# Loads of q, k and v of batches 1 to 3 by casting DMAs of GpSimd, in an attention and feed-forward kernel

## The chip, the cores and the metric

The kernel runs on one core of a Trainium2 chip. The metric is the device time of one execution in microseconds (us). The engines are named as the profile names them: PE multiplies matrices and transposes through the identity, DVE is the vector engine, ACT the scalar engine, POOL is GpSimd, SP only issues DMAs. A letter q behind a name (SPq) means the engine's instruction queue.

## The reference

Inputs are q, k, v of shape (4, 8, 768, 64) and two weight matrices, all float32. Attention is causal and keeps, for each query, the 6 chunks of 32 keys with the largest upper bound; its output goes through a feed-forward layer with softplus.

```python
k_min, k_max = k_chunks.min(axis=3), k_chunks.max(axis=3)       # 24 chunks of 32 keys
ub = np.sum(np.maximum(q * k_min, q * k_max), axis=-1)          # bound for each chunk
ub = np.where(causal, ub, -1e9)
top_chunks = np.argsort(ub, axis=-1)[..., -6:]
scores = q @ k.T / sqrt(64)
scores = np.where(sel & causal_pos, scores, -1e9)               # sel: chunk among the 6
attn = exp(scores - max) / sum
x = (attn @ v), heads side by side                              # (3072, 512)
out = softplus(x @ w_in) @ w_out                                # w_in (512, 2048), w_out (2048, 512)
```

## The kernel before

Work goes by units. A unit is a pair of heads with a range of query tiles of 128 rows: batch 0 has units 0 to 3 (first halves of the four pairs, 3 tiles) and 4 to 7 (second halves); batches 1 to 3 have units 8 to 19, one whole pair (6 tiles) each, so that unit u from 8 on is pair u - 4. For each unit there are small steps, and the whole order of these steps is written out by hand in the strings of ORDER (lines 21 to 60): "start" goes from the first load to the feed-forward input of batch 1, "cycle" is run twice, with the unit numbers raised by 4 the second time; steps of units over 19 fall away. There is no scheduler: each engine gets its instructions in the order of the text, takes them one after the other, and waits where it has to. The words that matter here:

- L8.k, L8.q, L8.v: load (line 165). Lu.c starts the DMA of one input of unit u. Units from 8 on bring 384 KB in one DMA on SP's queue (line 178) as float32 into a staging tile (three of each kind), in pieces of 64 numbers (256 bytes): for each of the 128 partitions 12 pieces, 6 tiles by 2 heads.
- ck, cq, cv: cast_k, cast_q, cast_v (lines 185 to 206). They turn the staging tile into bfloat16: k and q into kb and qb (three buffers each), v into a vaug tile. The letter behind it is the engine: V is DVE, A is ACT, G or nothing is GpSimd.
- vaug (line 113): five tiles that hold v as bfloat16 with a column of ones for the sums. Pair p uses tile p % 5, thus unit 8 (pair 4) and unit 13 (pair 9) use the same one.
- fk, fq: turn (line 212), a transposing DMA on SP's queue from kb or qb to kT_sb or qT_sb. kr, qr copy its rows into the operands Kaug and Qaug; rg, pk, qp, qn, U, M, T find the bounds and the selected chunks (DVE mostly), and s puts the selection into Qaug.
- S (scores, line 351): S8.1.0 is unit 8, head 1, group 0 of its score blocks: matmuls on PE, then Exp on ACT (line 366); for group 0 GpSimd then masks the diagonal blocks with an affine_select (line 369).
- V (values, line 373): V8.0 is unit 8, head 0: PE multiplies the weights attnT with vaug (line 383). n divides by the sums on DVE, X transposes on PE, x copies into xT.
- I and F: feed-forward input (line 413, softplus on ACT) and output (line 433). They are spread between the attention steps of the next batch and keep PE busy. ob copies the result to SBUF and stores it.
- w: the weights, in six casting DMAs that GpSimd issues (lines 446 to 453): w0 to w3 have 4 pieces of 512 numbers for each partition, w4 and w5 have 8.
- z: fills of two Sels tiles with zeros, and of the causal bias, on GpSimd.

The part of the order where units 8 and 9 meet unit 13 reads:

```python
I0.1.7 rg9.0 L12.v pk9 S8.0.0 qr9.0.V fq11 rg10.0 U9 ck11 tE S8.0.1 L13.k M9 T9 fk11 S8.0.2 rg10.1 L13.v ck12 s9 L13.q
kr10.0.A L14.q S8.1.0 kr9.0.A qp10 qn10 pk10 V8.0 F0.3.0 S8.1.1 U10 kr11.0.G M10 T10 n8.0 qr10.0.G S8.1.2 F0.3.1
```

Of the kernel before, what the change touches and what calls it, by code (L numbers as in the profile page):

```python
# [39 lines left out]
qn11 x8.A V9.0 kr11.1.A qp11 fk12 ck13 pk11 qr11.1.G S9.1.1 S9.1.2 n9.0 F0.3.3 fq12 U11 fk13 ob0.3.A M11 T11 L15.v  # L40
S10.0.0 V9.1 S10.1.0 n9.1 S10.0.1 s11 X9 cv13.V kr12.0.G qr12.0 qp12 rg12.0 rg12.1 L14.k S10.0.2 S10.1.1 qr12.1 pk12
V10.0 cq13.V S10.1.2 kr12.1.G L15.k S11.0.0 L15.q F0.4.1 S11.0.1 qn12 x9.V F0.4.2 fq13 S11.0.2 n10.0 U12 S11.1.0 V11.0
M12 S11.1.1 n11.0 V10.1 T12 F0.4.3 ck14.V S11.1.2 cq14.G n10.1 F0.5.0 s12 V11.1 F0.5.1 cv14.G tP n11.1 F0.5.2 X11 X10
F0.5.3 x11.V cv15.A ob0.4.A fk14 L16.q x10.V I1.-.0 I1.-.1 I1.-.2 qn13 rg13.0 I1.-.3 kr14.1.V fq14 L16.k L16.v I1.-.4
# [4 lines left out]
kr15.1.V kr15.0.G qp15 rg15.0 F1.0.0 rg15.1 qn15 pk15 qr15.1.V S12.0.0 cq16.V F1.0.1 S12.0.1 L18.v qr15.0.G L18.k  # L49
cv16.V F1.0.2 S12.0.2 F1.0.3 S12.1.0 U15 M15 S12.1.1 ob1.0.V V12.0 S12.1.2 ck16.V F1.1.0 n12.0 S13.0.0 V12.1 fk16  # L50
# [1 line left out]
kr16.1.V S13.1.2 F1.2.1 S14.0.1 ck18.A cv17.V V13.1 S14.0.2 n13.0 qp16 qr16.1.G n13.1 rg16.1 L19.v F1.2.2 F1.2.3 V14.0
ob1.1.A S14.1.0 pk16 ob1.2.V X13 kr16.0.V S15.1.0 n14.0 F1.3.0 cq17.A S14.1.1 F1.3.1 S14.1.2 F1.3.2 x13.A qn16 S15.0.0
F1.4.0 V14.1 U16 n14.1 S15.0.1 S15.0.2 ck17.V F1.3.3 fk18 fk17 M16 X14 cq18.G T16 x14.V F1.4.1 ob1.3.A L19.k S15.1.1
V15.0 L20.q n15.0 cv18.G S15.1.2 F1.4.2 L19.q F1.5.0 ck19.G V15.1 n15.1 qr16.0.A F1.4.3 L20.v rg18.1 F1.5.1 X15
# [1 line left out]
tP I2.-.4 rg18.0 I2.-.5 ob1.5.V L20.k fq18 s16 I2.-.6 U17 cq19.G qp18 qr18.1.V qr17.0.V I2.-.7 I2.-.8 I2.-.9 fk19 pk18
M17 I2.-.10 I2.-.11 qn18 T17 I2.-.12 U18 kr18.0 I2.-.13 fq19 cv19.A I2.-.14 I2.-.15 L21.q M18 kr18.1.V tE T18 L21.k
# [12 lines left out]
def kernel(  # L71
# [91 lines left out]
    SRC = {"k": k, "q": q, "v": v}  # L163

    def load(u, names="kqv"):
        p, t0, t1 = units[u]
        n = t1 - t0
        b, h0 = p // NPB, 2 * (p % NPB)
        for c in names:
            r = 4 if n < NT and c == "k" else n  # L170
            f = loads.tile([n * 128 // r, 2, r, D], F32, name=f"{c}f{n}", bufs=4 if n < NT else 3)
            src = SRC[c][b, h0:h0 + 2]
            if n < NT and c in "kq":

                nc.sync.dma_start(out=f.rearrange("p e t d -> p e (t d)"),
                                  in_=src[:, t0 * 128:t1 * 128].rearrange("e (s t) d -> s e (t d)", t=r))
            elif n == NT:
                nc.sync.dma_start(out=f.rearrange("p e t d -> p (e t) d"),
                                  in_=src.rearrange("e (t s) d -> s (e t) d", s=128))
# [4 lines left out]

    def cast_k(u, copy=nc.gpsimd.tensor_copy):
        p, t0, t1 = units[u]
        st = state[u]
# [3 lines left out]
        copy(st["kb"], st["kf"])

    def cast_q(u, copy=nc.gpsimd.tensor_copy):
        p, t0, t1 = units[u]
        st = state[u]
        if p < NPB:
            st["row"] = rows[p % 2][:, t0:t1]
            copy(st["row"][:, :, 1:3, :], st["qf"])
        else:
            st["qb"] = pairs.tile([128, t1 - t0, 2, D], BF16, name="qb", bufs=3)  # L200
            copy(st["qb"], st["qf"])

    def cast_v(u, copy=nc.gpsimd.tensor_copy):
        p, t0, t1 = units[u]
        pair[p]["va"] = vaugs[p % (SETS + 1)]
        copy(pair[p]["va"][:, t0:t1, :, 0:D], state[u]["vf"])
# [166 lines left out]
    def values(u, e):  # L373
        p, t0, t1 = units[u]
        st = state[u]
        at = st["at", e]
        off, groups = layout(u)
        n = t1 - t0
        o_ps = st["o", e] = ps_sm.tile([128, n, D + 1], F32, name="o_ps", tag="sm")
        for t in range(n):  # L380
            for tj in range(t0 + t + 1):
                o = off[(tj, t0 + t)]
                nc.tensor.matmul(o_ps[:, t, :], at[:, o:o + 128], pair[p]["va"][:, tj, e, :],  # L383
                                 start=(tj == 0), stop=(tj == t0 + t))
# [168 lines left out]
```

## Time and profile before

| what | value |
|---|---|
| three runs | 301.7, 301.86 and 303.8 us; median 301.86 us |
| the profiled execution's own time | its span, 299.2 us, plus what lies around it, which the page does not give |
| DVE, ACT busy | 171.4 and 197.9 us |
| DMA: SP's queue (q1) | 88768 packets, 29.89 MB |
| DMA: GpSimd's queue (q0) | 4192 packets, 4.19 MB |
| read from HBM | 27.26 MB |

The profile is of one execution, taken by the hardware. Its page gives the busy time of each engine, the chain of work that ended last (followed back from the last instruction), the groups of instructions, and the DMA issues with the time from issue to landing. The trace behind it can be asked for the rows of one engine in order of time: start, duration, engine, line, operation, output and input, count, and in square brackets how long the engine had been idle before and what it had waited for. Several instructions of one kind in a row are put together in one row.

### The profile page before, as it was taken

Reading aid. Unit: us, or ns where it says so; the run is one execution under the profiler, and the core shown is the slowest. Engines: PE = TensorE matmul, PEld = TensorE weight load, DVE = VectorE, ACT = ScalarE, POOL = GpSimd, SP = SyncE. Lnnn points to the kernel's source line nnn. Section 1 sums busy time; section 2 is a strip of 40 time slices with the busy share of each in tenths; the row PEclk is TensorE's granted clock in tenths of the full one; section 3 lists DMA queues with packets and bytes.
Section 4 is the critical chain, followed back from the end, with each engine's and each line's share of the span. In section 5 each row is a group of like instructions: output and inputs, shape, how many; then the busy total and the mean of one; then the engine's idle time right before and its main releaser. Section 6 shows DMA issues by size and latency. Waiting matters only on the chain.

```text
span 299.2 us, 6118 instructions
## 1 busy us (share of the span) xinstructions
PE 260.1 (87%) x2407; PEld 162.0 (54%) x2432; DVE 171.4 (57%) x572; ACT 197.9 (66%) x244; POOL 74.4 (25%) x104
## 2 busy tenths in 40 slices
PE   0385795789898797799999999999999999999994
PEld 0263553456455464556666666556666655665441
DVE  4986477985485799985459684646494313000000
ACT  1588549899756797655768788765786774567100
POOL 5035412433410665171013324112032120000000
PEclk9996599999999799999999999999999999999999
DMA  7989999916769998519395731932000101000111
GB/s 187 208 202 190 240 201 197 214 37 132 169 103 243 208 199 187 123 53 192 90 182 84 176 101 24 187 101 51 2 3 35 72 2 70 35 2 0 70 72 70
DMA packets 93628, 35.26 MB, mean 118 GB/s; under 512 B 82336, under 2 KB 90528, under 8 KB 93600
## 3 DMA queue, kind: packets, MB, share of 16 engines
q1 hardware_dynamic: 88768, 29.89, 47.9%
q0 software_dynamic: 4192, 4.19, 8.7%
q10 hardware_dynamic: 640, 0.79, 1.1%
q8 instruction: 19, 0.31, 0.5%
q14 instruction: 9, 0.07, 0.1%
HBM read 27.26 MB, written 6.29 MB: 112 GB/s over the span
## 4 chain that ended last, share of the span: by engine, by line
PE 62%; DVE 17%; ACT 10%; DMA 5%; issue 3%; SPq 1%; POOL 0%; ACTq 0%; DVEq 0%
PE hp L421 23%; PE op L437 21%; PE sc L362 8%; PE o_ps L383 6%; ACT attnT L366 4%; DVE km L234 3%; DMA vf<-in_v_dram 3%; ACT Kaug L248 2%; DMA kf<-in_k_dram 2%; DVE m L291 2%; PE x_ps L402 1%; DVE on L395 1%; DVE Kaug L248 1%; DVE kmm L240 1%; DVE Qaug L313 1%
## 5 line engine op out<-in xcount | busy, mean ns | idle before, releaser
L366 ACT ACTIVATE attnT<-sc 128x1024 bf16<-128x1024 f32 (+2 forms) x96 | 84.6, 917 | 23.0 <-PE sc L362 21.9
L437 PE MATMUL op<-w_out_sb,gT 128*128 128x512 bf16 x360 | 88.6, 381 | 1.4 <-issue 0.2
L421 PE MATMUL hp<-xT,w_in_sb 128*128 128x384 bf16 x512 | 87.0, 328 | 1.3 <-ACT attnT L366 1.3
L429 ACT ACTIVATE gT<-hp 128x768 bf16<-128x768 f32 x64 | 51.9, 810 | 38.6 <-PE hp L421 38.5
L421 PEld LDWEIGHTS <-w_in_sb 128*128 128x128 bf16 x512 | 49.9, 99 | 34.2 <-issue 2.7
L369 POOL TENSOR_SCALAR_AFFINE_SELECT attnT<-attnT 128x768 bf16<-128x768 bf16 (+1 forms) x40 | 29.4, 737 | 121.2 <-ACT attnT L366 121.1
L362 PE MATMUL sc<-Qaug,Kaug 128*128 128x128 bf16 (+3 forms) x399 | 53.1, 266 | 3.6 <-ACT attnT L366 2.1
L437 PEld LDWEIGHTS <-gT 128*128 128x128 bf16 x384 | 36.0, 98 | 35.0 <-issue 0.6
L362 PEld LDWEIGHTS <-Kaug 128*128 128x128 bf16 x400 | 30.3, 102 | 17.5 <-issue 4.0
L383 PE MATMUL o_ps<-vaug,attnT 128*128 128x65 bf16 x672 | 28.9, 198 | 4.5 <-ACT Qaug L313 2.0
L442 DVE COPY ob<-op 128x512 f32<-128x512 f32 x14 | 9.6, 686 | 40.0 <-PE op L437 39.8
L383 PEld LDWEIGHTS <-attnT 128*128 128x128 bf16 x672 | 26.7, 100 | 10.6 <-issue 3.1
L234 DVE TENSOR_REDUCE km<-kT_sb 128x24 bf16<-128x768 bf16 x24 | 22.2, 946 | 3.4 <-DMA kT_sb<-kb 3.2
L324 DVE COPY Qaug<-sT 64x768 bf16<-64x768 bf16 x24 | 13.3, 553 | 13.6 <-PE sT L321 13.4
L395 DVE TENSOR_TENSOR on<-o_ps,rr 128x384 bf16<-128x384 f32 (+1 forms) x40 | 19.1, 478 | 1.4
L394 DVE RECIPROCAL rr<-o_ps 128x6 f32<-128x6 f32 (+1 forms) x40 | 7.4, 184 | 20.5 <-PE o_ps L383 20.3
L281 DVE TENSOR_TENSOR ubm<-ub,causal 128x288 f32<-128x288 f32 (+2 forms) x20 | 7.5, 380 | 18.5 <-PE ub L279 18.2
L442 ACT COPY ob<-op 128x512 f32<-128x512 f32 x10 | 5.9, 585 | 17.2 <-PE op L437 17.2
L248 ACT COPY Kaug<-kT 64x384 bf16<-64x384 bf16 x12 | 11.8, 1024 | 7.5 <-DVE km L234 7.3
L291 DVE MAX8 m<-ubm 128x8 f32<-128x12 f32 (+3 forms) x192 | 16.4, 160 | 0.5
L278 PE MATMUL ub<-kmm,qpos 128*128 128x48 bf16 (+1 forms) x96 | 7.8, 184 | 6.2 <-DVE kmm L240 2.2
L410 ACT COPY xT<-x_ps 128x768 bf16<-128x768 bf16 (+1 forms) x11 | 7.6, 689 | 7.5 <-PE x_ps L402 7.4
(69 smaller groups left out, 243.5 us busy)
## 6 DMA issues: line engine op xcount, KB each, us to landing
out_dram<-ob SPq DMA_DIRECT2D x24, 256.0 KB, 2.1
kf<-in_k_dram SPq DMA_DIRECT2D x12, 384.0 KB, 6.1
vf<-in_v_dram SPq DMA_DIRECT2D x12, 384.0 KB, 5.4
qf<-in_q_dram SPq DMA_DIRECT2D x12, 384.0 KB, 5.4
w_in_sb<-in_moe_w_in_dram POOLq DMA_DIRECT2D x4, 512.0 KB, 8.0
w_out_sb<-in_moe_w_out_dram POOLq DMA_DIRECT2D x2, 1024.0 KB, 16.5
kf<-in_k_dram SPq DMA_DIRECT2D x8, 192.0 KB, 4.2
qf<-in_q_dram SPq DMA_DIRECT2D x8, 192.0 KB, 4.2
```

What stands on the lines that cost most here:

```text
L234: nc.vector.tensor_reduce(st["km2"][:, which, :], kT, axis=AX.XY, op=(ALU.max, ALU.min)[which])
L248: copy(o, kT)
L291: nc.vector.max(out=m8[:, t, e, :], in_=ubm[:, t, 0:max(8, 4 * (t + 1)) if n == NT else cs, e])
L362: nc.tensor.matmul(sc[:, o:o + (z - a) * 128], pair[p]["Ka"][e][:, tj * 128:(tj + 1) * 128], pair[p]["Qa"][e][:, a * 128:z * 128], start=T ...
L366: nc.scalar.activation(at[:, g * 1024:g * 1024 + n], sc[:, 0:n], ACT.Exp, scale=scale)
L369: nc.gpsimd.affine_select(out=diag, in_=diag, compare_op=ALU.is_ge, fill=0.0, base=0, channel_multiplier=-1, pattern=[[0, t1 - t0], [1, 128]])
L383: nc.tensor.matmul(o_ps[:, t, :], at[:, o:o + 128], pair[p]["va"][:, tj, e, :], start=(tj == 0), stop=(tj == t0 + t))
L395: nc.vector.tensor_tensor(st["on"][:, :, e, :], o_ps[:, :, 0:D], rr.to_broadcast([128, n, D]), op=ALU.mult)
L421: nc.tensor.matmul(hp[:, n, 0:HALF], w_in_sb[:, dt, ft * 128:(ft + 1) * 128], xT[b][:, dt, half * HALF:(half + 1) * HALF], start=(dt == 0) ...
L429: nc.scalar.activation(o, hp[:, :, 0:HALF], ACT.Softplus)
L437: nc.tensor.matmul(held[b, stt], gT[b][:, ft, stt * 128:(stt + 1) * 128], w_out_sb[:, ft, :], start=(ft == 0), stop=(ft == KFF - 1))
L442: copy(ob, held.pop((b, stt)))
```

## The change

Units 8 to 19 no longer go through staging tiles. Their load is issued by GpSimd at the place of the same L word, reads float32 and writes bfloat16: v in one DMA (12 pieces for each partition) straight into its vaug tile, whose layout becomes heads, tiles, columns; q and k in two DMAs, one for each head (6 pieces for each partition), into qb and kb, of which there are now five each. The 36 words ck, cq and cv of units 8 to 19 go out of ORDER (12 on DVE, 9 on ACT, 15 on GpSimd); every other word stays where it was. Units 0 to 7 load and cast as before.

```diff
-    vaugs = [singles.tile([128, NT, 2, D + 1], BF16, name=f"vaug{i}") for i in range(SETS + 1)]
+    vaugs = [singles.tile([128, 2, NT, D + 1], BF16, name=f"vaug{i}") for i in range(SETS + 1)]
...
         b, h0 = p // NPB, 2 * (p % NPB)
+        if n == NT:
+            for c in names:
+                if c == "v":
+                    pair[p]["va"] = vaugs[p % (SETS + 1)]
+                    nc.gpsimd.dma_start(out=pair[p]["va"][:, :, :, 0:D].rearrange("p e t d -> p (e t) d"),
+                                        in_=v[b, h0:h0 + 2].rearrange("e (t s) d -> s (e t) d", s=128))
+                    continue
+                f = state[u][c + "b"] = pairs.tile([128, NT, 2, D], BF16, name=c + "b", bufs=5)
+                for e in range(2):
+                    nc.gpsimd.dma_start(out=f[:, :, e, :],
+                                        in_=SRC[c][b, h0 + e].rearrange("(t s) d -> s t d", s=128))
+            return
...
-            elif n == NT:
-                nc.sync.dma_start(out=f.rearrange("p e t d -> p (e t) d"),
-                                  in_=src.rearrange("e (t s) d -> s (e t) d", s=128))
...
-        copy(pair[p]["va"][:, t0:t1, :, 0:D], state[u]["vf"])
+        copy(pair[p]["va"][:, :, t0:t1, 0:D].rearrange("p e t d -> p t e d"), state[u]["vf"])
...
-                nc.tensor.matmul(o_ps[:, t, :], at[:, o:o + 128], pair[p]["va"][:, tj, e, :],
+                nc.tensor.matmul(o_ps[:, t, :], at[:, o:o + 128], pair[p]["va"][:, e, tj, :],
                                  start=(tj == 0), stop=(tj == t0 + t))
```

In ORDER the two lines shown above become:

```python
I0.1.7 rg9.0 L12.v pk9 S8.0.0 qr9.0.V fq11 rg10.0 U9 tE S8.0.1 L13.k M9 T9 fk11 S8.0.2 rg10.1 L13.v s9 L13.q
kr10.0.A L14.q S8.1.0 kr9.0.A qp10 qn10 pk10 V8.0 F0.3.0 S8.1.1 U10 kr11.0.G M10 T10 n8.0 qr10.0.G S8.1.2 F0.3.1
```

The words L9.v, L13.v, L14.v, L15.v, L17.v, L18.v and L19.v stand ahead of the V words of units 4, 8, 9, 10, 12, 13 and 14, which read the same vaug tile. Before, the tile was written by the cast, which stood behind those V words. Now the load writes it, and these V words read the v of the later unit: this part of the computation is another one than before.

More of the change, by code (lines that the diff above doesn't have):

```diff
@@ L40 @@
[L40 to L44, printed above, removed]
@@ L45 @@
-qp14 I1.-.5 rg14.1 qn14 qp13 ob0.5.A rg14.0 I1.-.6 I1.-.7 rg13.1 pk14 I1.-.8 kr13.0.V I1.-.9 cq15.A ck15.G qr14.1.V
+S9.0.0 S9.0.1 V8.1 n8.1 qr10.1 F0.3.2 kr10.1.G rg11.0 S9.0.2 S9.1.0 s10 qr11.0.V rg11.1 X8 F0.4.0 L14.v
+qn11 x8.A V9.0 kr11.1.A qp11 fk12 pk11 qr11.1.G S9.1.1 S9.1.2 n9.0 F0.3.3 fq12 U11 fk13 ob0.3.A M11 T11 L15.v
+S10.0.0 V9.1 S10.1.0 n9.1 S10.0.1 s11 X9 kr12.0.G qr12.0 qp12 rg12.0 rg12.1 L14.k S10.0.2 S10.1.1 qr12.1 pk12
+V10.0 S10.1.2 kr12.1.G L15.k S11.0.0 L15.q F0.4.1 S11.0.1 qn12 x9.V F0.4.2 fq13 S11.0.2 n10.0 U12 S11.1.0 V11.0
@@ L46 @@
+M12 S11.1.1 n11.0 V10.1 T12 F0.4.3 S11.1.2 n10.1 F0.5.0 s12 V11.1 F0.5.1 tP n11.1 F0.5.2 X11 X10
+F0.5.3 x11.V ob0.4.A fk14 L16.q x10.V I1.-.0 I1.-.1 I1.-.2 qn13 rg13.0 I1.-.3 kr14.1.V fq14 L16.k L16.v I1.-.4
+qp14 I1.-.5 rg14.1 qn14 qp13 ob0.5.A rg14.0 I1.-.6 I1.-.7 rg13.1 pk14 I1.-.8 kr13.0.V I1.-.9 qr14.1.V
 pk13 U14 U13 I1.-.10 M14 I1.-.11 M13 L17.q I1.-.12 T14 kr14.0.V s14 fq15 T13 qr13.0 I1.-.13 I1.-.14 L17.v qr13.1.G
@@ L48 @@
 """, "cycle": """
[L49 to L50 removed]
+kr15.1.V kr15.0.G qp15 rg15.0 F1.0.0 rg15.1 qn15 pk15 qr15.1.V S12.0.0 F1.0.1 S12.0.1 L18.v qr15.0.G L18.k
+F1.0.2 S12.0.2 F1.0.3 S12.1.0 U15 M15 S12.1.1 ob1.0.V V12.0 S12.1.2 F1.1.0 n12.0 S13.0.0 V12.1 fk16
 S13.0.1 n12.1 L18.q F1.1.1 T15 F1.1.2 S14.0.0 F1.1.3 S13.0.2 fq16 X12 s15 S13.1.0 x12.A S13.1.1 F1.2.0 V13.0 rg16.0
[L52 to L55, printed above, removed]
+kr16.1.V S13.1.2 F1.2.1 S14.0.1 V13.1 S14.0.2 n13.0 qp16 qr16.1.G n13.1 rg16.1 L19.v F1.2.2 F1.2.3 V14.0
+ob1.1.A S14.1.0 pk16 ob1.2.V X13 kr16.0.V S15.1.0 n14.0 F1.3.0 S14.1.1 F1.3.1 S14.1.2 F1.3.2 x13.A qn16 S15.0.0
+F1.4.0 V14.1 U16 n14.1 S15.0.1 S15.0.2 F1.3.3 fk18 fk17 M16 X14 T16 x14.V F1.4.1 ob1.3.A L19.k S15.1.1
+V15.0 L20.q n15.0 S15.1.2 F1.4.2 L19.q F1.5.0 V15.1 n15.1 qr16.0.A F1.4.3 L20.v rg18.1 F1.5.1 X15
 kr17.1.A rg17.0 fq17 rg17.1 qn17 ob1.4.V F1.5.2 x15.A F1.5.3 qp17 I2.-.0 I2.-.1 qr17.1.V I2.-.2 pk17 kr17.0.A I2.-.3
[L57 to L58 removed]
+tP I2.-.4 rg18.0 I2.-.5 ob1.5.V L20.k fq18 s16 I2.-.6 U17 qp18 qr18.1.V qr17.0.V I2.-.7 I2.-.8 I2.-.9 fk19 pk18
+M17 I2.-.10 I2.-.11 qn18 T17 I2.-.12 U18 kr18.0 I2.-.13 fq19 I2.-.14 I2.-.15 L21.q M18 kr18.1.V tE T18 L21.k
 s18 qr18.0.G L21.v s17
@@ L168, in load @@
         b, h0 = p // NPB, 2 * (p % NPB)
+        if n == NT:
[10 more added lines that the diff above has]
+            return
         for c in names:
             r = 4 if n < NT and c == "k" else n
[L171 removed]
+            f = loads.tile([n * 128 // r, 2, r, D], F32, name=f"{c}f{n}", bufs=4)
             src = SRC[c][b, h0:h0 + 2]
@@ L195, in cast_q @@
         st = state[u]
[L196 to L201, printed above, removed]
+        st["row"] = rows[p % 2][:, t0:t1]
+        copy(st["row"][:, :, 1:3, :], st["qf"])
     def cast_v(u, copy=nc.gpsimd.tensor_copy):
```

14 lines of the change are left out of this document (6 added, 8 removed).

## The prediction

> **What bounds the kernel now.** I read the page's busy times and its chain first, then the busy time by stretch, then the rows of single engines around the steps that the change touches.
>
> ```profile
> span 299.2 us, 6118 instructions
> PE 260.1 (87%) x2407; PEld 162.0 (54%) x2432; DVE 171.4 (57%) x572; ACT 197.9 (66%) x244; POOL 74.4 (25%) x104
> PE 62%; DVE 17%; ACT 10%; DMA 5%; issue 3%; SPq 1%; POOL 0%; ACTq 0%; DVEq 0%
> ```
>
> PE is busy for 87% of the span and holds 62% of the chain that ended last; GpSimd is busy a quarter of the time and is not on the chain. The next view gives, for each stretch, its length, then busy time of PE, PE's weight loads, DVE, ACT and POOL, the granted PE clock, the DMA share and GB/s.
>
> ```profile
> 70.00:80.00 10.00, 9.52 (x109) 5.90 (x108) 4.49 (x12) 8.97 (x11) 3.10 (x5) 1.00 0.87 177
> 98.00:106.00 8.00, 6.66 (x68) 4.34 (x69) 6.45 (x34) 6.17 (x9) 5.19 (x6) 0.79 1.17 211
> 110.40:134.30 23.90, 19.54 (x262) 13.04 (x267) 22.06 (x67) 16.75 (x21) 12.18 (x14) 1.00 0.60 122
> 156.60:194.00 37.40, 37.00 (x408) 23.45 (x414) 26.90 (x77) 29.57 (x37) 11.38 (x13) 1.00 0.61 116
> 216.00:254.00 38.00, 37.59 (x409) 23.84 (x414) 17.59 (x50) 27.47 (x33) 7.72 (x9) 1.00 0.10 36
> ```
>
> The last two rows are the same cycle of steps, once with loads and casts (156.6 to 194) and once without (216 to 254): 37.4 and 38.0 us, PE full in both. So there the casts cost nothing now and their removal brings nothing. Only from 98 to 134 is PE not full, with DVE at 22.06 of 23.9 us in the main part: that is the one place where fewer casts can pay. PE takes its instructions in order, and from 134 on it is full to the end of these stages: whatever holds PE up is lost unless it closes another gap.
>
> **The parts, one by one.** Removed are 36 casts (12 on DVE, 9 on ACT, 15 on GpSimd) and 36 loads of SP. Added are 12 DMAs for v and 48 half-size ones for q and k, all issued by GpSimd, among its masks and copies. The price of one issue comes from the six casting DMAs that the kernel has already:
>
> ```profile
> 23.63 0.76 POOL L448 DMA_DIRECT2D w_in_sb<-in_moe_w_in_dram  x1
> 21.74 0.92 POOL L448 DMA_DIRECT2D w_in_sb<-in_moe_w_in_dram  x1
> 36.77 1.76 POOL L452 DMA_DIRECT2D w_out_sb<-in_moe_w_out_dram  x2
> ```
>
> By the code a w_in part has 4 pieces in each partition and a w_out part 8: 0.76 and 0.88 us, so 0.03 us for a piece more. A v load has 12 pieces (estimate 1.00 us), half a k or q load has 6 (0.82 us, 1.64 us for both halves). The bounds are 0.76 us whatever the count, and in proportion to it (0.19 us each: 2.28 and 1.14 us). I take the straight line, since it passes through both rows. GpSimd gets 12 x 1.00 + 48 x 0.82 = 51 us of issues for its 15 casts.
>
> How soon such a load lands is not shown for this shape. The nearest rows, issue to landing, first a hardware load alone on the queues, then the median of all v loads, then w_in amid other loads; then SP's own time to issue one, and the queues' packets:
>
> ```profile
> qf<-in_q_dram SPq DMA_DIRECT2D x1, 384.0 KB, 3.7
> vf<-in_v_dram SPq DMA_DIRECT2D x12, 384.0 KB, 5.4
> w_in_sb<-in_moe_w_in_dram POOLq DMA_DIRECT2D x3, 512.0 KB, 8.3
> 143.99 0.43 SPq L178 DMA_DIRECT2D qf<-in_q_dram  x1
> q1 hardware_dynamic: 88768, 29.89, 47.9%
> q0 software_dynamic: 4192, 4.19, 8.7%
> ```
>
> The 3.7 us hold 0.43 us of issue; with GpSimd's 1.00 us it is 4.3 us. I take 4.5 us where the queue is nearly empty and 5.0 us behind another load, with 3.7 and 8.3 us as ends. The Trainium skill ("DMA: Bandwidth & Descriptors", Anatomy of one DMA) fits a GpSimd DMA by 2.0 us plus its bytes over 436 GB/s: 2.9 us for such a load, and by that figure in all places the sum below would be +2.8 us instead of +7.9 us. This trace shows no 384 KB load under 3.7 us, so I stay with the rows.
>
> **The v loads.** This is what decides. A v load used to fill a staging buffer; a cast moved it into one of five vaug tiles later, when the tile was free. Now the load itself writes the tile, at the load's early place in the order. Seven of them (L9, L13, L14, L15, L17, L18, L19) stand ahead of the V steps that still read the tile for the pair five earlier. So those V steps wait on PE for a load that they have no need of. For each I ask when GpSimd comes to the load, and when PE wants the V step.
>
> V8.0 waits for L13.v, which stands behind the mask of S8.0.0 and the two halves of L13.k:
>
> ```profile
> 98.24 0.86 POOL L369 TENSOR_SCALAR_AFFINE_SELECT attnT<-attnT 128x768 bf16<-128x768 bf16 x1 [14.73 <-ACT attnT L366]
> 99.06 1.89 POOL L191 CAST kb<-kf 128x768 bf16<-128x768 f32 x2
> 101.86 0.91 POOL L369 TENSOR_SCALAR_AFFINE_SELECT attnT<-attnT 128x768 bf16<-128x768 bf16 x1 [0.92 <-ACT attnT L366]
> 100.40 1.36 PE L383 MATMUL o_ps<-vaug,attnT 128*128 128x65 bf16 x21
> ```
>
> The mask ends at 99.10, L13.k takes 1.64, L13.v lands 5.0 later: 105.74. V8.0 began at 100.40, so PE stands for 5.3 us. The next mask (S8.1.0) comes after L13.k, L13.v, L13.q and L14.q, at 99.10 + 1.64 + 1.00 + 3.28 = 105.0 instead of 101.86; its reader V8.1 is behind V8.0 and four score steps in PE's order, so this adds nothing.
>
> V9.0 waits for L14.v, which stands behind the mask of S9.1.0:
>
> ```profile
> 110.38 0.91 POOL L369 TENSOR_SCALAR_AFFINE_SELECT attnT<-attnT 128x768 bf16<-128x768 bf16 x1 [0.51 <-ACT attnT L366]
> 107.90 0.83 ACT L201 CAST qb<-qf 128x768 bf16<-128x768 f32 x1
> 110.44 0.80 PE L383 MATMUL o_ps<-vaug,attnT 128*128 128x65 bf16 x21 [0.24 <-DVE Qaug L324]
> ```
>
> 111.29 + 4.5 - 110.44 = 5.35 us, less about 0.7 of the 0.83 us of the cast of q12 on ACT, which stands in front of this exp: 4.6 us. It is measured from V8.0 on, so it comes on top. L15.v follows L14.v by one copy, and V10.0 only comes after S10's scores: no wait.
>
> V14.0 waits for L19.v, behind a copy of q rows:
>
> ```profile
> 172.40 0.83 POOL L267 COPY Qaug<-qT_sb 64x768 bf16<-64x768 bf16 x1
> 176.24 0.80 PE L383 MATMUL o_ps<-vaug,attnT 128*128 128x65 bf16 x21
> ```
>
> 173.23 + 4.5 - 176.24 = 1.5 us, in a stage where PE is full. V12 and V13 have their loads (L17.v, L18.v) well ahead, with whole score steps of other units between: nothing. V4.0 waits for L9.v, behind the first of two memsets:
>
> ```profile
> 51.84 1.41 POOL L488 MEMSET Sel<- 128x768 bf16 x2
> 56.90 0.62 PE L383 MATMUL o_ps<-vaug,attnT 128*128 128x65 bf16 x15
> 58.39 0.34 PE L312 MATMUL qa_ps<-ident,row 128*128 128x128 bf16 x3 [0.87 <-DVE row L300]
> ```
>
> 52.54 + 5.0 - 56.90 = 0.6 us, and PE idles 0.87 us right after: 0, at most 3.1 us at a landing of 8.3.
>
> **The casts that go.** First PE's waits from 110.3 to 134.3 and the casts on DVE there (of v13, q13, k14), then two earlier waits of PE:
>
> ```profile
> PE ub L278 <- DVE xT L410: 1.8, 1, 1.8
> PE sT L321 <- DVE Sel L300: 0.8, 1, 0.8
> PE ub L278 <- DVE kmm L240: 0.7, 1, 0.7
> 118.72 1.12 DVE L206 CAST vaug<-vf 128x768 bf16<-128x768 f32 x1
> 123.61 0.56 DVE L201 CAST qb<-qf 128x768 bf16<-128x768 f32 x1
> 128.36 1.17 DVE L191 CAST kb<-kf 128x768 bf16<-128x768 f32 x1
> 65.76 0.34 PE L312 MATMUL qa_ps<-ident,row 128*128 128x128 bf16 x3 [0.32 <-DVE row L300]
> 95.97 0.18 PE L278 MATMUL ub<-kmm,qpos 128*128 128x48 bf16 x1 [0.54 <-DVE kmm L240]
> ```
>
> DVE loses 2.85 us of casts, and while PE stands for V9.0 it works ahead. The three waits are 3.3 us, and the stretch has 23.9 - 19.54 = 4.4 us without PE in all. I take 3.0 us (0 to 4.4). Before 98 us, 0.5 of the 0.86 us of the two waits (0 to 0.9). Three casts of 0.83 us leave ACT between 67 and 74 us, but PE is busy there for 9.52 of 10 us with work that is next in its order: 0. SP's queue, shorter by 36 loads, hands transposes on sooner; none of PE's waits above is for one: 0.
>
> Sum: +5.3 + 4.6 + 1.5 - 3.0 - 0.5 = +7.9 us. The profiled span of 299.2 becomes 307.1 us. The median of the runs is 301.86, 2.7 us above that span, so the forecast is 309.8 us.
>
> The ends: at 3.7 us of landing the waits are 4.0 + 3.8 + 0.7, less 4.4 and 0.9: +3.2 us (305.1). At 8.3 us of landing with 1.14 us for each half of L13.k (V8.0: 99.10 + 2.28 + 8.3 - 100.40 = 9.3; V9.0 9.2; V14.0 5.3; V4.0 3.1) and nothing recovered: +27 us (329).
>
> **Rivals.** First, the casts' relief wins: faster. For it the load must land so soon that the V steps hardly wait, while all idle time of PE in the 98 to 106 row (1.3 us) and in the 110 to 134 row (4.4 us), and the 0.9 us before, goes. With a landing of L the waits are (L + 0.3) + (L + 0.1) + (L - 3.0, not under 0); to be 3 us faster they may be 1.3 + 4.4 + 0.9 - 3.0 = 3.6 us in all, so L at most 1.6 us, where it gives 298.9. With L of 3.7 it gives +1.9 us, 303.8. No row shows such a load under 3.7. Chance 0.04.
>
> Second, short landing, no change: L near 3.7 and most gaps closed: +2 to +3 us, about 304.5. For it: the load that was alone; against it: L13.v has L13.k in front and DMA at 1.17 of its engines around 98 to 106. Chance 0.12.
>
> Third, GpSimd's issues are held up by DVE. One issue took 0.92 against 0.76 us, and DVE is busy for 6.45 of 8 us from 98 to 106, with copies like this:
>
> ```profile
> 109.18 1.11 DVE L324 COPY Qaug<-sT 64x768 bf16<-64x768 bf16 x2
> ```
>
> If each issue waits for one such pair (1.1 us), L13.k and L13.v lose 3.3 us, L14.v and L19.v 1.1 each: +5.5 us more, 315. The Trainium skill ("SBUF — State Buffer", two separate sides) warns of it: while DVE runs in a mode with two ports, GpSimd can't write its descriptors. So far the six issues here show at most 0.16 us of it. Chance 0.18.
>
> Fourth, narrow packets drain slowly. GpSimd's queue took 8.7% x 299.2 x 16 / 4192 = 99 ns a packet, SP's 26 ns. A load is 1536 packets, 96 an engine: 9.5 us at 99 ns. L13.k and L13.v then land 2 x 9.5 - 5 = 14 us later than I take, and L14.v behind L13.q and L14.q some 15 to 20 us later again: about 340 us. Against it: those 99 ns packets carry eight times the data. Chance 0.08.
>
> **How the numbers follow.** Forecast as worked out (306 to 313 us): 0.58; its own range is 305 to 314. With 0.18 for the third, 0.08 for the fourth, 0.12 and 0.04 for the others. One per cent, about what a measurement can tell from no change, is 3.0 us: 304.9 is the border. Slower: 0.58 + 0.18 + 0.08 + 0.02 of the second case = 0.86; same 0.10; faster 0.04. The range from 304 to 321 leaves out the fourth case, the first, and some of the second.
>
> **What would show it.** Right: V8.0 and V9.0 wait on PE for a DMA into vaug, 5 us each, V14.0 for one or two; issues of v near 1.0 us and of halves near 0.82 us; PE's idle time behind V9.0 smaller; 216 to 254 unchanged in length. Wrong: no such wait of PE, or PE's idle time elsewhere; issues over 1.5 us; masks on GpSimd that V steps wait for; landings far from 4 to 5.5 us.

## The result, and the profile after

The changed kernel takes 320.57 us in the median of four runs (317.55 to 322.3), against 302.11 us for the kernel before on the same chip: 1.059 times as long, with a 95% interval from 1.052 to 1.066. The forecast was slower, 309.8 us in a range from 304 to 321. The direction is right and the time lies in the range, but the loss is 18.5 us where 7.9 were summed up. Medians are compared only with kernels run on the same chip in the same set of runs; the kernel before had medians from 301.35 to 302.75 us there. An execution over 1.5% above the fastest of its kernel counts as slow: the ratios leave it out, and so does the median of the changed kernel's second set of runs below (its slow execution took 322.35 us).

The page of the kernel after (its profiled execution took 317.55 us) gives busy times, the chain that ended last, and the two large queues.

```profile
span 315.8 us, 6120 instructions
PE 263.9 (84%) x2407; PEld 165.4 (52%) x2432; DVE 166.8 (53%) x560; ACT 192.3 (61%) x235; POOL 112.7 (36%) x149
...
q0 software_dynamic: 60448, 11.28, 45.7%
q1 hardware_dynamic: 32896, 15.74, 23.0%
...
PE 62%; POOL 8%; DMA 8%; issue 7%; DVE 7%; ACT 6%; SPq 1%; POOLq 0%; ACTq 0%; DVEq 0%
```

GpSimd, 0% of the chain before, now holds 8%, and DMA rose from 5% to 8%; DVE fell from 17% to 7%. DVE and ACT are busy for 4.6 and 5.6 us less, and yet the kernel is slower, so the place to look is what PE waits for. PE's waits, by what ended them (total, times, longest):

```profile
PE o_ps L388 <- DMA vaug<-in_v_dram: 11.5, 3, 5.2
...
PE x_ps L407 <- DVE on L400: 3.4, 2, 3.0
...
PE o_ps L388 <- POOL attnT L374: 2.0, 3, 1.1
```

The first row is the one that was foretold. The other two were not: a wait for DVE's norms ahead of a transpose (X), which was 0.67 us for X7 before, and waits for GpSimd's masks ahead of V steps, which the prediction lists among the signs that it would be wrong. PE's rows in order of time, at V8.0, V9.0 and V14.0 (start, length, and in brackets the wait), and GpSimd's from the mask of S8.0.0 to that of S8.1.0:

```profile
110.16 1.04 PE L388 MATMUL o_ps<-vaug,attnT 128*128 128x65 bf16 x16 [5.20 <-DMA vaug<-in_v_dram]
...
125.41 0.60 PE L388 MATMUL o_ps<-vaug,attnT 128*128 128x65 bf16 x8 [5.18 <-DMA vaug<-in_v_dram]
...
192.80 0.39 PE L388 MATMUL o_ps<-vaug,attnT 128*128 128x65 bf16 x7 [1.11 <-DMA vaug<-in_v_dram]
```

```profile
102.87 0.86 POOL L374 TENSOR_SCALAR_AFFINE_SELECT attnT<-attnT 128x768 bf16<-128x768 bf16 x1 [7.59 <-ACT attnT L371]
103.69 1.67 POOL L178 DMA_DIRECT2D kb<-in_k_dram  x2
105.33 1.10 POOL L173 DMA_DIRECT2D vaug<-in_v_dram  x1
106.41 3.31 POOL L178 DMA_DIRECT2D qb<-in_q_dram  x4
109.67 0.93 POOL L374 TENSOR_SCALAR_AFFINE_SELECT attnT<-attnT 128x768 bf16<-128x768 bf16 x1
```

L13.k takes 1.67 us behind the mask, L13.v is issued and V8.0 starts 4.83 us after the start of that issue: the order of events and the prices are those of the prediction. The mask (of S8.0.0) began at 98.24 before and begins at 102.87 now, though, so 4.6 us had been lost ahead of it. This table follows the loss through the two profiled executions:

| step on PE | start before | start after | later by |
|---|---|---|---|
| I0.0.6 (feed-forward input) | 50.28 | 50.53 | 0.3 |
| V7.1 | 78.82 | 81.06 | 2.2 |
| X7 | 80.40 | 84.71 | 4.3 |
| V8.0 | 100.40 | 110.16 | 9.8 |
| V9.0 | 110.44 | 125.41 | 15.0 |
| I1, first step | 134.28 | 149.03 | 14.8 |
| V14.0 | 176.24 | 192.80 | 16.6 |
| I2, first step | 193.91 | 210.58 | 16.7 |

From 216 to 254 the cycle without loads took 38.0 us; its counterpart here takes 38.1 us. The next rows are of the changed kernel: V8.0 to V9.0, V9.0 to I1 (the two stretches that should have won something), and the counterpart of the cycle without loads (length, then PE, weight loads, DVE, ACT, POOL, PE's clock, DMA share, GB/s).

```profile
110.16:125.41 15.25, 9.79 (x104) 6.43 (x106) 9.33 (x29) 6.70 (x8) 7.49 (x9) 0.84 0.80 72
125.41:149.03 23.62, 21.50 (x261) 14.87 (x266) 17.00 (x58) 14.91 (x18) 15.78 (x19) 0.88 0.88 78
232.62:270.72 38.10, 37.69 (x410) 23.99 (x414) 17.47 (x49) 27.36 (x33) 7.71 (x9) 1.00 0.10 36
```

DVE's load from V9.0 to I1 fell from 22.00 to 17.00 us and PE's idle time from 4.3 to 2.1 us, yet the stretch is as long as before (23.62 against 23.84 us). PE is busy for 2 us more with the same matmuls, at a mean clock of 0.88 instead of 1.00.

### The profile page after: what moved, and what is told of

Read it like the earlier page. It is cut to its first block, busy times and chain, and to the rows that moved or that the text cites. A ratio compares the mean times of both kernels' runs of the same rounds, so it can differ in the third digit from the quotient of the medians.

```text
span 315.8 us, 6120 instructions
## 1 busy us (share of the span) xinstructions
PE 263.9 (84%) x2407; PEld 165.4 (52%) x2432; DVE 166.8 (53%) x560; ACT 192.3 (61%) x235; POOL 112.7 (36%) x149
## 3 DMA queue, kind: packets, MB, share of 16 engines
q0 software_dynamic: 60448, 11.28, 45.7%
## 4 chain that ended last, share of the span: by engine, by line
PE 62%; POOL 8%; DMA 8%; issue 7%; DVE 7%; ACT 6%; SPq 1%; POOLq 0%; ACTq 0%; DVEq 0%
PE hp L426 23%; PE op L442 20%; PE sc L367 8%; PE o_ps L388 6%; DMA vaug<-in_v_dram 4%; ACT attnT L371 2%; POOL attnT L374 2%; DMA qT_sb<-qb 2%; POOL kb L178 2%; DMA kf<-in_k_dram 2%; DVE km L239 1%; PE x_ps L407 1%; ACT Qaug L318 1%; ACT Kaug L253 1%; POOL vaug L173 1%
## 5 line engine op out<-in xcount | busy, mean ns | idle before, releaser
L442 PE MATMUL op<-w_out_sb,gT 128*128 128x512 bf16 x360 | 89.5, 384 | 1.4 <-issue 0.2
L367 PE MATMUL sc<-Qaug,Kaug 128*128 128x128 bf16 (+3 forms) x399 | 54.7, 271 | 5.4 <-ACT attnT L371 3.5
L388 PE MATMUL o_ps<-vaug,attnT 128*128 128x65 bf16 x672 | 30.3, 200 | 17.0 <-DMA vaug<-in_v_dram 11.5
L367 PEld LDWEIGHTS <-Kaug 128*128 128x128 bf16 x400 | 31.2, 104 | 19.6 <-issue 5.8
L388 PEld LDWEIGHTS <-attnT 128*128 128x128 bf16 x672 | 28.1, 102 | 23.4 <-issue 14.5
L178 POOL DMA_DIRECT2D qb<-in_q_dram x24 | 19.9, 844 | 0.0
L178 POOL DMA_DIRECT2D kb<-in_k_dram x24 | 19.9, 838 | 0.0
L272 POOL COPY Qaug<-qT_sb 64x768 bf16<-64x768 bf16 x10 | 8.7, 873 | 22.3 <-DMA qT_sb<-qb 22.0
L296 DVE MAX8 m<-ubm 128x8 f32<-128x12 f32 (+3 forms) x192 | 16.4, 160 | 0.5
```

Of the source, the lines that this page charges most:

```text
L178: nc.gpsimd.dma_start(out=f[:, :, e, :], in_=SRC[c][b, h0 + e].rearrange("(t s) d -> s t d", s=128))
L296: nc.vector.max(out=m8[:, t, e, :], in_=ubm[:, t, 0:max(8, 4 * (t + 1)) if n == NT else cs, e])
L367: nc.tensor.matmul(sc[:, o:o + (z - a) * 128], pair[p]["Ka"][e][:, tj * 128:(tj + 1) * 128], pair[p]["Qa"][e][:, a * 128:z * 128], start=T ...
L442: nc.tensor.matmul(held[b, stt], gT[b][:, ft, stt * 128:(stt + 1) * 128], w_out_sb[:, ft, :], start=(ft == 0), stop=(ft == KFF - 1))
```

## The experiments

The profiled executions of all kernels reach I0.0.6 between 49.1 and 53.7 us, over code that is nearly the same. So stretches are compared from that step on. This is how much later than before each step starts, with I0.0.6 set equal:

| run | time (before), us | V7.1 | V8.0 | V9.0 | I1 | I2 |
|---|---|---|---|---|---|---|
| changed kernel | 320.57 (302.11) | 2.0 | 9.5 | 14.7 | 14.5 | 16.4 |
| the same, again | 320.12 (302.67) | 2.0 | 9.5 | 14.8 | 14.2 | 16.0 |
| v as before | 303.25 (302.75) | 1.1 | 1.4 | 1.9 | -0.2 | 0.0 |
| only v | 320.83 (302.75) | 1.3 | 7.0 | 13.0 | 13.2 | 15.9 |
| 16 tiles | 306.52 (302.75) | 2.0 | 5.0 | 5.9 | 4.0 | 5.3 |
| v late | 304.63 (302.75) | 0.4 | 3.5 | 3.9 | 2.0 | 2.8 |
| PE busy while it waits | 316.51 (302.67) | 2.4 | 10.5 | 13.8 | 12.1 | 15.0 |
| only L14.v late | 313.19 (302.67) | 2.0 | 10.0 | 10.1 | 8.2 | 10.7 |
| 16 tiles, loads packed early | 306.1 (302.67) | 6.1 | 5.5 | 5.0 | 3.5 | 4.8 |
| 16 tiles, masks free | 307.08 (301.98) | 0.2 | 5.9 | 5.0 | 3.5 | 4.5 |
| 16 tiles, transposes free | 303.15 (301.35) | 2.0 | 0.5 | 1.1 | -0.2 | 1.3 |
| 16 tiles, both free | 300.93 (301.98) | 0.2 | -0.2 | -0.8 | -2.4 | -0.9 |
| both free, more moved | 298.97 (301.35) | 1.4 | 0.3 | -0.1 | -1.6 | -1.6 |

**Which part costs: v, or q and k?** The theory was that PE's waits for v are about 12 of 17 us; the rivals, that GpSimd's issues are most of it, or its narrow packets. The first kernel takes the v part back (load by SP, staging, cast), the second has the v part alone.

```diff
-                    pair[p]["va"] = vaugs[p % (SETS + 1)]
-                    nc.gpsimd.dma_start(out=pair[p]["va"][:, :, :, 0:D].rearrange("p e t d -> p (e t) d"),
-                                        in_=v[b, h0:h0 + 2].rearrange("e (t s) d -> s (e t) d", s=128))
+                    f = loads.tile([128, 2, NT, D], F32, name="vf6", bufs=3)
+                    nc.sync.dma_start(out=f.rearrange("p e t d -> p (e t) d"),
+                                      in_=v[b, h0:h0 + 2].rearrange("e (t s) d -> s (e t) d", s=128))
+                    state[u]["vf"] = f.rearrange("p e t d -> p t e d")
```

The words cv of units 8 to 19 stand where they stood before. The second kernel has the lines taken out here and the new layout of vaug, and in all else the code of the kernel before, with the words ck and cq.

> q and k by casting DMAs, v of units 8 to 19 again by SP, staging tile and cast at the old place. Theory 1 (the V steps wait for v loads that stand too early; this cost about 12 of the 17 us, and the rest, about 4.5 us, comes up to 95 us from loads issued by GpSimd ahead of masks and beside transposes): the three waits of PE for vaug are gone, 304 to 307 us, S8.0.0 on PE at 97 to 99 us. Rival A (GpSimd's issues as such hold up its masks and copies everywhere; 39 of the 52 us of issues remain): 313 to 316 us. Rival B (narrow packets of GpSimd's queue crowd out everything else; two thirds of them remain): 311 to 315 us.

It took 303.25 us, 1.004 times the time before (1.001 to 1.008), a little less than the theory's 304 to 307, and no PE wait for vaug is left.

> Only v by casting DMAs, at the early places; q and k as before. Theory 1: V8.0 waits about 3.5 us (L13.k no longer in front), V9.0 5 us, V14.0 1.4 us, nothing lost before 95 us: 311 to 314 us. Rival A (12 us of issues left of 52): 304 to 307 us. Rival B (a third of the packets): 306 to 309 us.

It took 320.83 us, 1.065 times (1.058 to 1.072): above what any of the theories had expected, and as much as the whole change. Its waits:

```profile
PE o_ps L388 <- DMA vaug<-in_v_dram: 12.9, 3, 5.7
```

So the v part is nearly all of the loss, and q and k by themselves cost about 1 us. The three waits were longer than expected: 4.70, 5.70 and 2.50 us at V8.0, V9.0 and V14.0, where 3.5, 5 and 1.4 had been put down. From V9.0 to I1 nothing comes back (24.0 us). 3 us of the profiled span arose before I0.0.6, and for them I have no cause.

**Is it the shared tile?** Two kernels keep every load on GpSimd and take away only PE's waits for v: 16 tiles instead of five, or five tiles with the v loads at the old places of the casts. In both each V reads its own v.

```diff
-    vaugs = [singles.tile([128, 2, NT, D + 1], BF16, name=f"vaug{i}") for i in range(SETS + 1)]
+    vaugs = [singles.tile([128, 2, NT, D + 1], BF16, name=f"vaug{i}") for i in range(NP)]
...
-                    pair[p]["va"] = vaugs[p % (SETS + 1)]
+                    pair[p]["va"] = vaugs[p]
```

> As changed, but with sixteen vaug tiles, one for each pair, so that no load writes a tile that V steps still read (the V steps read their own v again). Theory 1: no wait of PE for vaug, only what is lost before 95 us stays: 303 to 307 us. Rivals A and B: all issues and packets are as in the changed kernel, 313 to 320 us.

306.52 us, 1.016 times (1.010 to 1.022): of the 18.5 us, 14.7 are gone with the waits for vaug and what follows them. The waits for DVE and for masks are still there:

```profile
PE x_ps L407 <- DVE on L400: 4.0, 3, 3.5
...
PE o_ps L388 <- POOL attnT L374: 3.8, 5, 1.1
```

The other one, of whose moves two are shown (parts of lines of ORDER):

```diff
-fk11 S8.0.2 rg10.1 L13.v s9 L13.q
+fk11 S8.0.2 rg10.1 s9 L13.q
...
-S10.0.0 V9.1 S10.1.0 n9.1 S10.0.1 s11 X9 kr12.0.G
+S10.0.0 V9.1 S10.1.0 n9.1 S10.0.1 s11 X9 L13.v kr12.0.G
...
-X8 F0.4.0 L14.v
+X8 F0.4.0
...
-V11.1 F0.5.1 tP
+V11.1 F0.5.1 L14.v tP
```

> As changed, five vaug tiles, but the words L8.v to L19.v stand where the casts cv8 to cv19 stood, behind the V steps that read the tile's former content (the V steps read their own v again). Theory 1: no needless wait, 303 to 307 us like the sixteen tiles. If instead the loads then come too late for their own V steps, PE waits for vaug at V8 to V11: 308 us or more. Rivals A and B: 313 to 320 us.

304.63 us, 1.011 times (1.005 to 1.017), with no wait for vaug either.

**Why did the missing casts give nothing back?** After the second wait PE's clock was half. Two stretches of the changed kernel, the wait ahead of V8.0 and the time from V9.0 on:

```profile
104.00:110.00 6.00, 0.96 (x7) 0.70 (x8) 2.57 (x6) 3.14 (x4) 6.00 (x8) 0.50 1.48 96
125.40:131.00 5.60, 5.37 (x49) 3.72 (x51) 1.38 (x6) 2.20 (x3) 0.00 (x0) 0.50 0.32 21
```

The granted clock is 0.50 in both. The trace has it at 0.50 from 103.9 to 114.1 us and from 124.3 to 131.2 us, and in the kernel before from 100.3 to 103.7 us:

```profile
103.90:114.00 10.10, 4.66 (x38) 3.07 (x40) 2.67 (x6) 3.24 (x4) 8.28 (x10) 0.50 1.63 121
100.30:103.60 3.30, 3.08 (x28) 1.96 (x27) 2.66 (x7) 2.30 (x3) 1.78 (x3) 0.50 0.97 159
```

So at V8.0 the clock had fallen 1.1 us before the wait began (104.96), as it had before the change; the wait only kept it down for 10.2 us instead of 3.4. At V9.0 the wait, from 120.2 us on, brought it down. The Trainium skill ("TensorE: Matmul & The Clock Gate", Part 1: The HAM clock gate) says that PE's clock falls to half after an idle window of about 3.4 us and comes back after a busy one, and that these windows run on without regard to the kernel. The trace agrees at V9.0: the clock fell 4.1 us into the wait, and the half clock lasted 6.8 us, two times 3.4, of which 5.8 lay behind the start of V9.0. At V8.0 PE was busy for 1.35 of the 3.4 us before the clock fell, so that fall was not behind a fully idle stretch.

The next kernel gives PE something to do while it waits; the results of these 32 matmuls are overwritten.

```diff
+        if (u, e) in ((8, 0), (9, 0)):
+            for _ in range(16):
+                nc.tensor.matmul(o_ps.rearrange("p t d -> p (t d)"), ident, w_in_sb[:, 0, 0:n * (D + 1)],
+                                 start=True, stop=True)
```

> The changed kernel, with 16 matmuls of 390 columns (the identity times a part of w_in, results overwritten) in front of V8.0 and again in front of V9.0. They need nothing that is late, so PE works through most of the two waits of 5.2 us instead of standing. In the changed kernel the granted clock was 0.50 from 104 to 114 and from 125.4 to 131 us, and the stretch from V9.0 to the feed-forward input I1 took 23.6 us, 23.9 before, although V9.0's wait had let DVE work ahead. Theory A (the half clock ate what the missing casts gave): the clock is near 1.00 behind V9.0, the stretch takes 21.5 to 22.5 us, and the kernel is 1.5 to 3 us faster than the changed one, about 317. Theory B (DVE and the order bound that stretch, the clock changes only how PE's time is divided between work and standing): the stretch still takes 23.2 us or more, and the kernel is within 1 us of the changed one in the same call.

> The changed kernel as it is, once more on this chip, for the comparisons of this call: 316 to 321 us. Both theories: V8.0 and V9.0 wait 5 us each for a v load, V9.0 to I1 takes 23.3 to 23.9 us. If that stretch differs by more than 0.5 us from the first profile, the 23.6 us there are chance and the clock can't be judged by it.

316.51 us against 320.12 us for the changed kernel beside it, 3.6 us less. V8.0 to V9.0 and V9.0 to I1 with PE kept busy:

```profile
112.34:125.69 13.35, 10.96 (x121) 7.05 (x123) 9.32 (x29) 6.70 (x8) 7.80 (x9) 1.00 1.10 85
125.69:147.80 22.11, 20.64 (x262) 14.23 (x266) 16.78 (x58) 14.91 (x18) 15.75 (x19) 0.92 0.88 81
```

The first is 1.9 us shorter, at a clock of 1.00; the second is 1.1 to 1.5 us shorter (23.62 and 23.19 us in the two profiles of the changed kernel), at 0.92, since the matmuls there end 2.1 us before the load lands. Together 3.0 to 3.4 us were the half clock. The profiled executions don't keep all of it: V8.0 came 1.0 us later in this one, and I1 to I2 took 1.1 us more, so that 1.0 us is left at I2, and both spans are 315.6 us. The gain rests on the stretches and on the medians.

**Do the waits add up?** Only L14.v moves, behind V9.1 and V11.1, where the cast of v14 had been (parts of lines).

```diff
-X8 F0.4.0 L14.v
+X8 F0.4.0
...
-V11.1 F0.5.1 tP
+V11.1 F0.5.1 L14.v tP
```

> The changed kernel, with only L14.v moved, to the place where the cast of v14 used to stand, behind V9.1: V9.0 has nothing to wait for, V8.0 and V14.0 keep their waits. Theory A (each wait costs itself, and the clock after it a little more): V9.0's wait of 5.2 us is gone and the stretch from V9.0 to I1 gets what PE's clock lost, so the kernel is 5 to 7 us faster than the changed one: 312 to 315. Theory B (the waits are not additive, V9.0 would then wait for the mask or the selection that comes as late): 316 or more. If V8.0's wait does not cost anything by itself: 308 or less.

313.19 us, 6.9 us less than the changed kernel beside it; the profiled spans differ by 5.4 us. V9.0 no longer waits, and from there to I1:

```profile
120.89:142.80 21.91, 19.43 (x262) 13.11 (x266) 19.58 (x64) 15.63 (x20) 18.09 (x22) 1.00 1.11 92
```

At the full clock the stretch takes 21.91 us instead of 23.84: the casts that went are worth 1.9 us here, where PE doesn't come out of a wait. So the wait of 5.2 us at V9.0 costs itself and takes most of what would have been won behind it.

**What is left over the time before?** With 16 tiles 4 us remain. They arise before V8.0, where this kernel is 5.0 us late; with only q and k on GpSimd it was 1.4 us, and with only v 2.3 us (7.0 less the wait of 4.70). Two things differ there: GpSimd's issues stand in front of masks, and its loads run beside SP's transposes. GpSimd's rows ahead of the mask of S5.0.0, in the changed kernel:

```profile
61.06 1.04 POOL L173 DMA_DIRECT2D vaug<-in_v_dram  x1
62.09 1.65 POOL L178 DMA_DIRECT2D kb<-in_k_dram  x2
63.73 1.03 POOL L374 TENSOR_SCALAR_AFFINE_SELECT attnT<-attnT 128x384 bf16<-128x384 bf16 x2
```

That mask had started at 60.92; L8.v and L9.k stand in front of it now, and V5.0 waits 1.06 us for it. Then DVE's and PE's rows at X7, after, and behind them DVE's row of the kernel before:

```profile
82.96 0.95 DVE L239 TENSOR_REDUCE km<-kT_sb 128x24 bf16<-128x768 bf16 x1 [6.00 <-DMA kT_sb<-kb]
...
84.71 0.34 PE L407 MATMUL x_ps<-ident,on 128*128 128x128 bf16 x3 [3.02 <-DVE on L400]
```

```profile
77.95 0.95 DVE L234 TENSOR_REDUCE km<-kT_sb 128x24 bf16<-128x768 bf16 x1 [3.22 <-DMA kT_sb<-kb]
```

PE's X7 needs the norm n7.1 from DVE, and DVE stands in front of it for a transposed k (rg9.1). The transposes issued from 74 to 86 us in the kernel before:

```profile
kT_sb<-kb SPq DMA_TRANSPOSE x2, 3.9
qT_sb<-qb SPq DMA_TRANSPOSE x2, 2.6
```

GpSimd's queue and the same transposes in the kernel after, from 74 to 90 us:

```profile
q0 software_dynamic: 5862, 0.74, 77.8%
...
kT_sb<-kb SPq DMA_TRANSPOSE x2, 6.8
qT_sb<-qb SPq DMA_TRANSPOSE x2, 6.4
```

The last number of a transpose is the median time from issue to landing in us. GpSimd's packets take 77.8% of the 16 DMA engines' time in this window; before there were none, and SP's queue took 69.7% of it. The Trainium skill ("DMA: Bandwidth & Descriptors", Issuing engines are not separate DMA queues) says that DMAs of all issuing engines run on the same 16 engines and interleave; these rows agree.

A first attempt, from the kernel with 16 tiles, moved the loads to places where GpSimd had been idle, packing those of units 8 and 9 behind the last weights (here and below, parts of ORDER):

```diff
-w5 tE L8.k kr5.1.A
+w5 tE L8.k L9.k L8.q L9.q L8.v L9.v kr5.1.A
...
-L12.v pk9 S8.0.0
+L12.v L13.k L13.v pk9 S8.0.0
```

Beside these, q and k of unit 10 go to the old places of L8.q and L9.q, L10.v behind L11.v, L13.q behind qr10.0.G and L14.q behind kr10.1.G.

> Sixteen vaug tiles as in the run with 16 tiles, where each V reads its own v and 306.5 us were measured, and besides the loads of units 8 to 10 and 13 and q of 14 stand at places where GpSimd had been idle: those of units 8 and 9 right behind the last weights, none directly in front of a mask, three fewer beside the transposes of k8 to q9. Theory A (what was left over the time before came from issues in front of masks and from loads beside transposes): PE's waits for masks, 3.8 us in the run with 16 tiles, shrink below 1.5, I1 starts at 135 to 137 instead of 138.4, and the time is 300 to 304. Theory B (the price is GpSimd's 51 us of issues beside DVE's copies, wherever they stand): mask waits may shrink but DVE is as late, and the time stays at 305 to 308.

306.1 us, as theory B had it, but not for its reason. GpSimd itself had stopped:

```profile
41.59 1.69 POOL L178 DMA_DIRECT2D qb<-in_q_dram  x2
48.29 0.82 POOL L178 DMA_DIRECT2D qb<-in_q_dram  x1 [5.00 <-DMA w_out_sb<-in_moe_w_out_dram]
53.36 0.82 POOL L178 DMA_DIRECT2D qb<-in_q_dram  x1 [4.25 <-DMA w_out_sb<-in_moe_w_out_dram]
```

Each of the two issues waited for the weight DMA eight issues ahead of it to land: in the trace GpSimd's DMAs use eight semaphores in turn, and these two carry a wait for the semaphore that they use themselves. The cast of q6 behind them came late, and PE stood 4.3 us for it (V7.1 is 6.1 us late in the table). From there to V8.0 it lost nothing more, where 16 tiles lost 3.0 us. The next three kernels put no more than six such DMAs behind the weights, and tell the two kinds apart.

From the kernel with 16 tiles, the masks free:

```diff
+w5 tE L8.k L9.k
...
+V5.1 S6.1.0 L8.v n5.1
...
+V6.0 S7.0.0 L9.v fk8
...
+L12.v L13.k L13.v pk9 S8.0.0
...
+qr10.0.G L13.q S8.1.2
...
+kr10.1.G L14.q rg11.0
```

and the transposes free; the third has both:

```diff
+w5 tE L8.k L8.q
...
+cq7.G L9.q S4.1.0
...
+rg7.0 L10.q rg7.1 X4 L10.k qn7
...
+pk8 L11.v L10.v U8
```

> The run with 16 tiles (306.5 us), with only those loads moved that stood right in front of a mask: k of unit 9 goes behind k of unit 8 (the last weights' issues), v of 8 behind the mask of S6.1.0, v of 9 behind that of S7.0.0, k and v of 13 ahead of the mask of S8.0.0, q of 13 and 14 behind two copies. Everything else, with the loads of q8, q9 and of unit 10 beside the transposes from 74 to 92 us, stays. Theory A (both cost: issues in front of masks some 2 us, loads beside transposes some 2 us): V5.0's second part no longer waits for its mask (1.06 us), the two waits of V8.1 and V9.0 for masks (0.86 and 0.91 us) go, X7 is still 2 us late, and the time is 303.5 to 305. Theory B (only the masks count): 301.5 to 303. Theory C (only the transposes count): 306 or more.

> As the run before this one, and the loads of q8, q9 and unit 10 are moved away from the transposes too: q8 behind k9, q9 behind the cast of q7, q and k of 10 to the old places of q8 and q9, v of 10 behind v of 11. Unlike in the run with the loads packed behind the weights, no more than 6 casting loads follow the weights, so that the two waits of GpSimd there (5.00 and 4.25 us, for the weights' DMAs to land) and PE's wait of 4.3 us for the cast of q6 should not come back. Theory A: no wait for masks over 0.6 us, X7 no later than before, I1 at 132 to 134, and 299 to 302, that is 1 to 3 us under the time before: the missing casts then bring 2 us and little is lost. Theory B (only the masks count): the same as the run before within 0.7 us. If 9 casting DMAs in a row already fill what the queue holds: a wait of GpSimd for the weights again, and 303 or more.

> The run with 16 tiles (306.5 us), with only the loads moved that landed beside the transposes of k8 to q9 (q of 8 and 9, q, k and v of 10, to the places that they had in the run of 300.93 us); the loads in front of masks stay. Freeing the masks alone had changed nothing (307.1), freeing both had given 300.93. Theory A (the two sit one behind the other: DVE stands for the transposes of k9, and the time that the masks cost is hidden behind that as long as it lasts): X7's wait of 3.5 us shrinks to 1 to 2 us, V5.0 and the masks of S8.1.0 and S9.1.0 are as late as with 16 tiles (waits of about 1 us each), and the time is 302.5 to 305. Theory B (only the transposes cost): 300.5 to 301.5. Theory C (only both together help): 306 or more.

Masks free alone: 307.08 us, 1.016 times (1.013 to 1.020), no gain; theory A of that run, which had both cost by themselves, is wrong. V7.1 came 1.8 us earlier, but X7 waited for the same transposes, 4.42 us against 3.52 with 16 tiles, and at V8.0 nothing is left of the gain.

```profile
84.54 0.50 PE L407 MATMUL x_ps<-ident,on 128*128 128x128 bf16 x3 [4.42 <-DVE on L400]
```

Transposes free alone: 303.15 us, 1.007 times (1.004 to 1.009); from 74 to 90 us transposes landed after 5.1 us (k) and 2.8 us (q) there, and PE's longest wait for a norm is 0.7 us. Both: 300.93 us, 0.997 times (0.994 to 1.0005), and X7's wait there is

```profile
82.30 0.34 PE L407 MATMUL x_ps<-ident,on 128*128 128x128 bf16 x3 [1.64 <-DVE on L400]
```

So the two delays lie one behind the other: the masks' 2 us are covered by the transposes' delay as long as that lasts, and count once it is gone (2.2 us at I1 and I2, between the rows "transposes free" and "both free" of the table). The last kernel moves more loads of the same two kinds.

```diff
+cq7.G L9.q L8.v S4.1.0
...
+V5.1 S6.1.0 L9.v n5.1
...
+kr13.1.G L16.q L16.k fk15 s13 qr14.0.G L16.v L17.q L17.v L17.k tE
...
+S12.1.0 L18.k U15
```

> The run of 300.93 us with a few more loads moved away from transposes and masks: v of 8 and 9 earlier (X7 there still waited 1.64 us), q, k and v of 16 and q and v of 17 behind the transposes of k14 and q13, which took 7 us to land there (a wait of 0.68 us for kmm), k of 18 behind the mask of S12.1.0 (a wait of 0.43 us). Theory A (what is left are waits of the same two kinds): these three waits shrink by 1 to 2.2 us together and the time is 298.8 to 300, 2 to 3 us under the time before. Theory B (what is left is DVE's and PE's own work): 300.5 to 301.5, the same as before the move.

298.97 us, 0.992 times the time before (0.989 to 0.995): the first version that is faster than the kernel before, by 2.4 us. X7 waits 0.67 us in it, as before the change. All 60 of GpSimd's issues and all its loads are still there, so neither costs anything here by its number; what cost was where they stood.

## Why the prediction was right in direction and too small

The prediction failed at the step that put nothing down for what GpSimd's loads delay ahead of V8.0, and at the size of what the missing casts give back. That 320.57 us lies inside the range is luck: that part of the range, 314 to 321, was there for issues held up by DVE, which did not come.

**V8.0 waits for L13.v, +5.3; V9.0 for L14.v, +4.6; V14.0 for L19.v, +1.5.** Right: 5.2, 5.2 and 1.1 us. The run with 16 tiles shows that these waits, with what they bring along, are over three quarters of the loss. The prices under them were right too; the page of the kernel after:

```profile
kb<-in_k_dram POOLq DMA_DIRECT2D x24, 96.0 KB, 3.8
vaug<-in_v_dram POOLq DMA_DIRECT2D x12, 192.0 KB, 4.6
qb<-in_q_dram POOLq DMA_DIRECT2D x24, 96.0 KB, 4.2
```

A v load landed after 4.6 us in the median, where 4.5 and 5.0 were taken (L13.v 4.8 and L14.v 4.5, but L12.v, issued beside transposes at 94.2 us, 11.2); an issue took 1.05 us for v and 0.84 us for a half of k or q, where the straight line through the weights' rows gave 1.00 and 0.82. By the 2.9 us of the Trainium skill ("DMA: Bandwidth & Descriptors", Anatomy of one DMA) the waits at V8.0 and V9.0 would have been 1.6 to 1.9 us shorter than they were; the measurement decides. The third and fourth rivals are refuted: none of the twelve v issues took more than 1.16 us, and a packet of GpSimd's queue took 45.7% x 315.8 x 16 / 60448 = 38 ns, not 99.

**"I take 3.0 us (0 to 4.4)"** for the casts between 110 and 134 us. Failed by its size: 0.2 us came back (0.6 in the second profile). It assumed that PE, once its operand had landed, would go on as before with less to wait for. The kernel with only L14.v moved shows 1.9 us for the casts at the full clock, and the one with PE kept busy shows that the half clock after the waits took 1.1 to 1.5 us behind V9.0 and 1.9 us behind V8.0. The latter was no loss against the kernel before, which ran V8.0 to V9.0 at 0.84 as well. The prediction had the clock in its rows (0.79 around V8.0, where PE already stood before) and did not ask what a wait of 5 us leads to.

**"Before 98 us, 0.5", and for SP's queue "none of PE's waits above is for one: 0".** This is the step that failed most: +4.6 us at the mask of S8.0.0 instead of -0.5. The prediction priced GpSimd's 51 us of issues, and then followed only those in front of a v load and of one mask (S8.1.0). It did not ask which mask stands behind which issue there (S5.0.0 behind L8.v and L9.k), nor what SP's transposes share with GpSimd's loads. Looking for PE's waits for a transpose was the wrong question: DVE waited for one already (3.22 us before), and PE stood behind DVE. The runs show the two causes: with the transposes free V8.0 is 0.5 us late instead of 5.0, and with the masks free too it is not late.

**"nothing" for V12 and V13.** V12.1 waits 0.4 us for a mask behind an issue; +0.5 us. The cycle without loads kept its length, as said.

In sum: 4.6 ahead of V8.0, 5.2 + 5.2 for V8.0 and V9.0, less 0.2, then 0.5 for V12, 1.3 around V14.0 and 0.1 behind it make 16.7 us of shift at I2, and the profiled spans differ by 16.6 us. The medians differ by 18.5, as executions of the changed kernel reach 322.3 us; I can't say which stretch makes the slower ones slower.

## What to carry to other kernels

When a load starts to write its final operand, its place in the order has to move to where the cast was, or the operand needs more buffers: ask of every moved write which reader of the old contents stands behind it. When DMA issues move to an engine that also computes, list for each issue what is queued behind it, and for each load which transfers share its engines; such delays can cover each other, so that undoing one shows nothing. A wait of PE of about 5 us is to be priced with the half clock that follows it, as far as the clock was not half there already.

## What the hardware showed that was not expected

- PE's clock fell to 0.50 4.1 us into a wait of 5.2 us and stayed there for 6.8 us, 5.8 of them behind the wait; 16 matmuls of 390 columns put into such a wait had it back at 1.00 when V8.0 began, and shortened the loss at V9.0.
- DMA transposes slow down beside GpSimd's casting loads: 3.9 and 2.6 us became 6.8 and 6.4 us. Whether the narrow pieces or the casting do it was not tried.
- With eight DMAs of GpSimd on their way, its next issue waited until the first of them had landed (5.00 and 4.25 us); GpSimd's copies and masks stood behind it. The wait is the program's, for one of eight semaphores; what the chip itself would allow is not shown.
